# One attention unit inside a fused attention and two-layer MLP kernel: its own place table, a third softmax buffer, and products of zeros ahead of its local scores

## The chip, the cores and the metric

The program runs on one core of one Trainium2 chip. The metric is device microseconds of one execution. The kernel before was timed three times: median 927.83 us, from 927.24 to 928.4. One more execution was taken with the hardware profiler: 926.6 us, of which the span from its first to its last instruction is 924.7 us. All rows below come from that execution.

## The reference

Inputs are `q`, `k`, `v` of shape (4, 8, 576, 64) and four float32 weight matrices. The attention has a part over means of 4 positions, repeated 4 times, and a part over a band of 7 positions. Two gated MLPs follow, on 2304 tokens of 512 features with 2048 hidden features.

```python
def attn(q, k, v):                       # B=4, H=8, S=576, D=64
    q_d, k_d, v_d = (a.reshape(B, H, S // 4, 4, D).mean(axis=3) for a in (q, k, v))
    out_up = np.repeat(sm_attn(q_d, k_d, v_d), 4, axis=2)
    mask = np.abs(pos[:, None] - pos[None, :]) < 4
    scores = np.where(mask, scale * q @ k.T, -1e9)
    out_local = softmax(scores) @ v
    return out_up + out_local

x = attn(q, k, v)                        # as 2304 x 512
h = x @ w1_in;  x = (h * sigmoid(h)) @ w1_out
h = x @ w2_in;  out = (h * clip(h + 3, 0, 6) / 6) @ w2_out
```

## The kernel before, in words

The 2304 tokens are cut into eight units of 288 (half a batch element each). A matrix product in float32 is made of three products of split operands: each operand is a high part and a low part in a reduced form of float32, and high x high, low x high and high x low are added. The splitting costs ScalarE (ACT, the high part by a cast), VectorE (DVE) and GpSimd (POOL, the low part by a subtraction).

**First layer.** A row `f` (a block of 128 hidden features, 16 in all) of a unit is `gemm1` (tile `h`, 12 products of 288 columns), then `gate1` (ACT and DVE, tile `t`), then `split_g` (ACT `gh`, POOL `gl`), and two rows later `y_unit1` (tile `y`, 12 products into four accumulators). The first two units are run in an odd order: unit 0 rows 0 to 7, unit 1 rows 0 to 15, unit 0 rows 8 to 15. The four accumulators `ys` are the four buffers of the PSUM pool `ps_y`. All other products, those of attention too, go through the four buffers of `ps_w`.

**Weights.** While these first passes run, the weights of the first layer are still arriving and are converted on the chip: per tile of 128x1024 words, ACT makes `wu`, POOL or ACT makes `wt`, DVE joins them (`wt<-wu,wt`), ACT casts the high part `w` and POOL subtracts the low part (`w<-wt,w`). One conversion step is issued per place in the row loop, behind the marks of an earlier row (`gates`). The MLP products need these tiles in order.

**Attention of the next unit, listed by places.** Each row `f` has two places (`nxt[2 * i]` behind `split_g`, `nxt[2 * i + 1]` behind the `y` products). `attention(u, n, at, ...)` fills them from a table: `ATT` for units 1 and 2, `ATT_LATE` for later ones, with `at` turning a table position into a place. The pieces are: `ls` local scores (32-column products, tile `ls`), `le` and `ln` the local softmax, `lt` and `lp` its transposes into `xo`, `ds`/`dx`/`dn` scores and softmax of the mean part (tiles `ds`, `de`, `dr`), `dt` its transposes (`deT`), `dv` its values (`od`), and `lv` the local values with the final sum `x`. Unit 1's attention runs over unit 0's rows 0 to 7, that is over 16 places; before, by `ATT` with

```python
    first_att = attention(1, 2 * HF, lambda p: 1 + p * 12 // 22)
```

so that `ls` stood in places 1 and 2, `dt` in 5 to 9, `dv` in 7 and 9, `lv` in 10, 11 and 13. At row 7 `split_x` makes unit 1's operand `xhl` from `x`.

**Buffers.** Softmax results `de` and their transposes `deT` of unit 1 share the tag `de` with three buffers. The tag `stg` has two buffers; unit 0 uses them for `leT`, unit 2 for its `q` and `k` loads (`qkraw`).

**What sets the order.** The framework's scheduler orders each engine's instructions by a simulated timeline within the limits the program sets (`issue_after`, `behind`, `in_line`). An engine then runs its list strictly in order. All loads and stores are issued on SyncE's queue (SP), in order too: an issue that waits for a buffer holds back those behind it. Line 31 is the recording helper through which ACT, DVE and POOL instructions go, line 339 the one for products.

**Products of zeros.** In the prologue `keep_warm` puts products of a tile of zeros (tile `idle`) between attention pieces. The kernel before has none after the prologue.

Of the kernel before, what the change touches and what calls it, by code (L numbers as in the profile page):

```python
# [8 lines left out]
F32 = mybir.dt.float32  # L9
F32R = mybir.dt.float32r  # L10
U32 = mybir.dt.uint32
BF16 = mybir.dt.bfloat16
# [26 lines left out]
def attention_moe_moe2_kernel(  # L39
# [11 lines left out]
    nc = tc.nc  # L51
# [3 lines left out]
    P = 128  # L55
    NC = DM // P
    NF = DFF // P
    UT = S // 2
# [3 lines left out]
    SD = S // FACTOR  # L62
    UD = UT // FACTOR
# [9 lines left out]
    pool = ctx.enter_context(tc.tile_pool(name="pool", bufs=1))  # L73
# [18 lines left out]
    def parts(tag, *shapes):  # L92

        sizes = [a * b for a, b in shapes]
        t = pool.tile([P, sum(sizes)], F32, tag=tag, name=tag, bufs=1)
        at = [sum(sizes[:i]) for i in range(len(sizes))]
        return [t[:, i:i + a * b].rearrange("p (a b) -> p a b", a=a) for i, (a, b) in zip(at, shapes)]

    kT, qT, kd = parts("xe", (NC, KW), (NC, QW), (NC, SD))
# [236 lines left out]
    latest = [None]  # L336
# [4 lines left out]
    def in_line():  # L341

        return tc.issue_after(latest[0])
# [102 lines left out]
    def down_scores(u, ch):  # L446

        ss = []
        own = u == 0 and ch == 1
        for par in range(2):  # L450
            ps = (ps_y if own else ps_w).tile([P, 512], F32, tag="y" if own else "w", name="ds")
            ss.append(ps[:UD, :2 * SD].rearrange("p (c j) -> p c j", c=2))
        for c in range(2):
            for par in range(2):
                rows = slice(64 * par, 64 * par + 64)
                mm(
                    ss[par][:, c, :], qd[rows, 2 * ch + c, :], kd[rows, 2 * ch + c, :],
                    start=True, stop=True,
                )
        return ss  # L460

    def down_exp(u, i, s):
        m = pool.tile([UD, 2, 1], F32, tag="dm", name="dm", bufs=4)
        vec.tensor_reduce(out=m, in_=s, axis=AX.X, op=ALU.max)
        sc = scale / (FACTOR * FACTOR)
        vec.tensor_scalar(out=m, in0=m, scalar1=-sc, scalar2=None, op0=ALU.mult)
        if u == 0:
            e = pool.tile([UD, 2, SD], F32, tag=("gh", "gl")[i % 2], name="de", bufs=2)
        else:
            e = pool.tile([UD, 2, SD], F32, tag="de" if u < 3 else "wt", name="de", bufs=3)  # L470
        r = pool.tile([UD, 2, 1], F32, tag="dr", name="dr", bufs=4)
        for c in range(2):
            act.activation(e[:, c, :], s[:, c, :], AF.Exp, bias=m[:, c, :], scale=sc, accum_out=r[:, c, :])
        return e, r

    def down_norm(eng, e, r):
        vec.tensor_scalar(
            out=r, in0=r, scalar1=EPS, scalar2=float(FACTOR), op0=ALU.add, op1=ALU.mult
        )
        vec.reciprocal(r, r)  # L480
        eng.tensor_tensor(out=e, in0=e, in1=r.to_broadcast([UD, 2, SD]), op=ALU.mult)
# [72 lines left out]
    def local_spread(par, t, a, turning=False):  # L554

        rows = slice(32 * a, 32 * a + 32)
        copy = act.copy if a % 2 or turning else vec.tensor_copy
        copy(pT[rows, par * NC * G:(par + 1) * NC * G, QB * a:QB * (a + 1)], t[rows, :, 0:QB])
# [20 lines left out]
    def split_x0(g):  # L579
# [4 lines left out]
        act.copy(hi, s)  # L584
        vec.tensor_tensor(out=lo, in0=s, in1=hi.bitcast(F32), op=ALU.subtract)

    xs = {}
    NPOS = 2 * NF

    def attention_calls(u):  # L590

        st = {}
        local_engines = ((vec, vec), (gps, gps), (vec, vec))[min(u, 2)]
        down_engines = (gps, gps)

        def begin():
            st["od"] = pool.tile([P, NC, UD], F32, tag="od", name="od", bufs=1)
            if u == 0:
                xhl[0] = pool.tile([P, 2, NC, UT], F32R, tag="xhl", name="xhl", bufs=1)
                xs[0] = st["x"] = pool.tile([P, NC, UT], F32, tag="x32", name="x32", bufs=1)  # L600

        def ds(ch): st["ds", 2 * ch], st["ds", 2 * ch + 1] = down_scores(u, ch)
        def dx(i): st["e", i] = down_exp(u, i, st["ds", i])
        def dn(i): down_norm(down_engines[i // 2], *st["e", i])
        def dt(i): st["eT", i] = down_transpose(st["e", i][0])
        def dv(ch): down_values(u, ch, [st["eT", 2 * ch + par] for par in range(2)], st["od"])
        def ls(c): local_scores(u, st.setdefault("ls", []), c)
        def le(i): st["le", i] = local_exp(local_engines[i], u, st["ls"][i])
        def ln(i): local_norm(local_engines[i] if u else vec, st["le", i])
        def lt(i): st["leT", i] = local_transpose(u, st["le", i])  # L610
        def lp(i, a): local_spread(i, st["leT", i], a, u == 0 and i == 0)
        def lv(g):
            if u and g == 0:
                xs[u] = st["x"] = pool.tile([P, NC, UT], F32, tag="x32", name="x32", bufs=1)
            local_values(u, g, st["od"], st["x"])

        return dict(begin=begin, ds=ds, dx=dx, dn=dn, dt=dt, dv=dv, ls=ls, le=le, ln=ln, lt=lt, lp=lp, lv=lv)

    VALUES = (1, 3, 5, 7, 9, 11, 16, 18)

# [3 lines left out]
    def attention(u, n, at, ahead=None, after=17):  # L624

        names = attention_calls(u)
        places = [[] for _ in range(n)]
        first = at(0)
        for p, calls in (ATT_LATE if u > 2 else ATT).items():
            for name, *args in calls:  # L630
                places[at(p)].append((names[name], args))
        if u == 1:
            for i in range(4 * G):
                places[0].append((load_vw, (u, i // 4, i % 4)))
        if u > 1:
            prep = []
            if u % 2 == 0:
                for i in range(NC):
                    prep += [[(load_qk, (u, i)), (prep_k, (i,)), (prep_q, (i,))]]
                for h in range(H):  # L640
                    prep += [[(load_vd, (u // 2, h)), (prep_vd, (u // 2, h))]]
            else:
                prep = [[(load_qk, (u, i)), (prep_q, (i,))] for i in range(NC)]
            if u == 2:

                for p, calls in zip((10, 12), prep):
                    places[p].append((held, calls[:1]))
                for p, calls, then in zip(THIRD, prep, prep[2:] + [[], []]):
                    places[p].append((held, calls[1:] + then[:1]))
                prep = []  # L650
            start = 0
            if ahead is not None:

                for i in range(NC):
                    load, *turns = prep.pop(0)
                    ahead[after + 3 * i].append(load)
                    ahead[after + 3 + 3 * i].append((queued, turns))
                for i, (load, turn_v) in enumerate(prep):
                    if i < 2:
                        ahead[30 + i].append(load)  # L660
                    else:
                        places[VALUES[i - 2]].append(load)
                    places[VALUES[i]].append((queued, [turn_v]))
                prep = []
            for i, calls in enumerate(prep):
                places[start + i * (first - start) // len(prep)].append((held, calls))
            for i in range(4 * G):
                places[i * first // (4 * G)].append((load_vw, (u, i // 4, i % 4)))
        return places
# [11 lines left out]
    def held(*calls):  # L681
# [3 lines left out]
    ATT = {  # L685
        0: [("begin",), ("ls", 0)],
        1: [("ls", 1)],
        2: [("ls", 2)],
        3: [("ls", 3)],
        4: [("le", 0)],  # L690
        5: [("le", 1), ("ds", 0)],
        6: [("dx", 0), ("dx", 1), ("ln", 0)],
        7: [("dn", 0), ("ln", 1)],
# [11 lines left out]
        22: [("lv", 2)],  # L705
    }


    ATT_LATE = {
        0: [("begin",), ("ls", 0)],  # L710
# [223 lines left out]
    def split(i):  # L934
        split_w(0, *order[i])
        done.add((0, *order[i]))

    names = attention_calls(0)
    def keep_x():
        nc.sync.dma_start(x0d, xs[0])  # L940
# [93 lines left out]

    HF = NF // 2
    passes = [(0, range(HF)), (1, range(NF)), (0, range(HF, NF))] + [(u, range(NF)) for u in range(2, NU)]
    first_att = attention(1, 2 * HF, lambda p: 1 + p * 12 // 22)
    for c in range(2, NC):
        first_att[0].insert(0, (late_q, (c, qn1[c // 2])))
    first_att[0].sort(key=lambda call: call[0] is not late_q)  # L1040
# [13 lines left out]

    for n_pass, ((u, fs), nxt) in enumerate(zip(passes, nxts)):
        ys = [ps_y.tile([P, 512], F32, tag="y", name="y") for _ in range(NC)]
        ys = [y[:, :UT] for y in ys]
        x = xhl[u]
        end = {0: end_half1, 2: end_half2}.get(n_pass, end_unit1)
# [149 lines left out]
    for at in range(n_q):  # L1209
        u, p = divmod(at, HP)  # L1210
        n = sizes[u]
# [72 lines left out]
```

## Time and profile before

| | |
|---|---|
| median of 3 runs | 927.83 us (927.24 to 928.4) |
| profiled execution | 926.6 us, its span 924.7 us |
| PE busy | 902.3 us, 98% of the span |
| PE weight loads busy | 830.1 us, 90% |
| DVE, ACT, POOL busy | 481.9, 415.4, 351.0 us |
| share of PE on the chain that ended last | 89% |

A busy PE is not a PE at its peak: its instructions are pipelined, and its clock has two levels, 2.4 GHz (granted clock 1.00 in the rows) and 1.2 GHz (0.50). What a wait or a slow clock is worth has to be read in the stretch where it stands, since an engine that catches up later gives nothing to the end. Idle time is shown in brackets behind a row, with the engine and tile whose signal came last.

### The profile page before, as it was taken

How to read it: one execution, taken by the hardware profiler on the slowest of the kernel's cores; microseconds unless marked ns; L12 is line 12 of the kernel's file. 1: busy time of each engine (PE TensorE's matmuls, PEld its weight loads, DVE VectorE, ACT ScalarE, POOL GpSimd, SP SyncE). 2: the span in 40 equal slices, each digit the busy share in tenths (PEclk: the TensorE clock that was granted, in tenths of full speed). 3: DMA queues.
4: the chain of work that ended last, by engine and by line, in shares of the span. 5: the costliest groups of instructions: out<-in, count | busy, mean ns of one | idle time of the engine just before them, and what ended most of it. 6: DMA issues, size and time to landing. Idle time of an engine off the chain costs nothing.

```text
span 924.7 us, 20977 instructions
## 1 busy us (share of the span) xinstructions
PE 902.3 (98%) x8231; PEld 830.1 (90%) x8231; DVE 481.9 (52%) x986; ACT 415.4 (45%) x973; POOL 351.0 (38%) x457
## 2 busy tenths in 40 slices
PE   7989899999999999999999999999999999999998
PEld 4778798999999999999999998888898888888896
DVE  4874368455455364643634655555446444644422
ACT  5678635335444354443534554343325224322432
POOL 6678952225464353663346633341006003200100
PEclk9889999999999999999999999999999999999999
DMA  8979653535857758565359997667658656754580
GB/s 207 301 228 284 200 125 84 125 93 145 254 173 207 198 158 242 184 203 187 132 187 354 382 363 211 183 206 229 180 168 252 191 173 182 238 175 145 162 271 23
DMA packets 218474, 185.07 MB, mean 200 GB/s; under 512 B 90120, under 2 KB 200968, under 8 KB 218376
## 3 DMA queue, kind: packets, MB, share of 16 engines
q1 hardware_dynamic: 218376, 183.74, 65.8%
q8 instruction: 65, 1.06, 0.5%
q14 instruction: 33, 0.27, 0.1%
HBM read 154.21 MB, written 29.49 MB: 199 GB/s over the span
## 4 chain that ended last, share of the span: by engine, by line
PE 89%; DVE 4%; POOL 3%; ACT 2%; issue 1%; DMA 1%; SPq 0%; POOLq 0%; ACTq 0%; DVEq 0%
PE y L339 41%; PE h L339 20%; PE m L339 19%; PE lv L339 2%; PE ls L339 2%; PE idle L783 1%; PE dv L339 1%; PE ds L339 1%; PE dt L346 1%; PE nt L339 1%; DMA wcd<-chi 1%; POOL wt L31 1%; POOL w L31 1%; ACT t L31 0%; DVE xo L31 0%
## 5 line engine op out<-in xcount | busy, mean ns | idle before, releaser
L339 PE MATMUL h<-xhl,w 128*128 128x288 f32 x1536 | 230.9, 300 | 3.2 <-DVE t L31 1.3
L339 PE MATMUL y<-gh,w 128*128 128x288 f32 x1024 | 226.1, 298 | 1.5 <-ACT gh L31 0.5
L339 PEld LDWEIGHTS h<-xhl,w 128*128 128x128 f32 x1536 | 211.2, 190 | 8.8 <-DVE t L31 1.7
L339 PE MATMUL y<-w,g 128*128 128x512 f32 x864 | 215.7, 397 | 0.9 <-DVE g L31 0.5
L339 PEld LDWEIGHTS y<-w,g 128*128 128x128 f32 x864 | 156.3, 188 | 35.1 <-DVE g L31 2.4
L339 PEld LDWEIGHTS y<-gh,w 128*128 128x128 f32 x1024 | 171.0, 189 | 4.2 <-ACT t L31 1.2
L31 DVE SCALAR_TENSOR_TENSOR t<-t,h 128x288 f32<-128x288 f32 (+1 forms) x192 | 101.7, 532 | 128.4 <-ACT t L31 127.9
L31 POOL TENSOR_TENSOR gl<-t,gh 128x288 fp32r<-128x288 f32 x112 | 93.5, 835 | 181.6 <-ACT gh L31 167.3
L339 PE MATMUL y<-gl,w 128*128 128x288 f32 x512 | 149.6, 298 | 3.6 <-POOL qkraw L31 1.5
L339 PEld LDWEIGHTS y<-gl,w 128*128 128x128 f32 x512 | 96.3, 188 | 4.7 <-POOL qkraw L31 1.7
L31 ACT ACTIVATE t<-h 128x288 f32<-128x288 f32 x128 | 52.2, 408 | 98.7 <-PE h L339 88.4
L31 ACT CAST gh<-t 128x288 fp32r<-128x288 f32 x128 | 55.4, 433 | 85.4 <-PE y L339 62.1
L339 PEld LDWEIGHTS m<-xa,ring 128*128 128x128 f32 x720 | 90.2, 188 | 3.4
L339 PE MATMUL m<-xa,ring 128*128 128x256 f32 x720 | 91.9, 279 | 0.0
L339 PEld LDWEIGHTS m<-xb,ring 128*128 128x128 f32 x624 | 78.5, 188 | 4.1 <-DVE h L31 0.4
L31 ACT ACTIVATE t<-m,three 128x256 f32<-128x256 f32 x48 | 22.8, 474 | 129.9 <-PE m L339 126.5
L339 PE MATMUL m<-xb,ring 128*128 128x256 f32 x624 | 80.0, 280 | 0.0
L31 POOL TENSOR_TENSOR w<-wt,w 128x512 fp32r<-128x512 f32 x48 | 61.9, 1301 | 43.6 <-ACT w L31 37.0
L31 DVE SCALAR_TENSOR_TENSOR t<-t,m 128x256 f32<-128x256 f32 x48 | 20.2, 421 | 110.1 <-ACT t L31 110.1
L31 POOL TENSOR_TENSOR xa<-xsum,xa 128x512 fp32r<-128x512 f32 x9 | 12.1, 1343 | 151.9 <-ACT xa L31 151.9
L31 DVE TENSOR_TENSOR g<-t,g 128x512 fp32r<-128x512 f32 (+1 forms) x80 | 60.1, 759 | 6.2 <-ACT g L31 3.0
L31 ACT ACTIVATE t<-h,three 128x256 f32<-128x256 f32 x64 | 36.0, 610 | 41.3 <-DVE h L31 41.2
(96 smaller groups left out, 1035.3 us busy)
## 6 DMA issues: line engine op xcount, KB each, us to landing
ring<-wcd SPq DMA_DIRECT2D x120, 512.0 KB
w<-wsd SPq DMA_DIRECT2D x44, 512.0 KB
raw<-in_moe_w_out_dram SPq DMA_DIRECT2D x32, 512.0 KB
raw<-in_moe_w_in_dram SPq DMA_DIRECT2D x16, 512.0 KB
craw<-in_moe_w_in_dram SPq DMA_DIRECT2D x32, 256.0 KB
sevenths<-wcd SPq DMA_DIRECT2D x32, 256.0 KB
wcd<-chi SPq DMA_DIRECT2D x16, 448.0 KB
wcd<-comb SPq DMA_DIRECT2D x16, 448.0 KB
```

Of the source, the lines that this page charges most:

```text
L31: r = getattr(self.engine, name)(*args, **kwargs)
L339: latest[0] = nc.tensor.matmul(*args, **kwargs).ins
L346: latest[0] = nc.tensor.transpose(*args).ins
L783: nc.tensor.matmul(ps[:, :n_cols], z[:, :P], z[:, :n_cols], start=True, stop=True)
```

## The change

Unit 1 gets a table of its own, `ATT_FIRST`, whose positions are places as they are (`lambda p: p`). `ls`, `le`, `ds 0`, `dx 0`, `dx 1`, `ln` keep the places they had. `dx 2` moves from 5 to 6, `dx 3` from 7 to 6, `dt` from 5, 6, 8, 9 to 6, 7, 9, 10, `dv` from 7, 9 to 9, 11, `lv` from 10, 11, 13 to 12, 13, 13. Unit 1's softmax results 2 and 3 go into the two buffers of `stg`. Ahead of the first `ls`, seven products of 224 columns are issued on a zero column of `kT`, which is read as bf16 and broadcast; they write columns 288 to 511 of the first accumulator's PSUM buffer, which nothing else uses.

```diff
         if u == 0:
             e = pool.tile([UD, 2, SD], F32, tag=("gh", "gl")[i % 2], name="de", bufs=2)
+        elif u == 1 and i > 1:
+            e = pool.tile([UD, 2, SD], F32, tag="stg", name="de", bufs=2)
         else:
...
+        def fill(n):
+            z = kT[:, 0, 0:1].bitcast(BF16)[:, 0:1]
+            with in_line():
+                for _ in range(n):
+                    latest[0] = nc.tensor.matmul(
+                        spare[0], z.to_broadcast([P, P]), z.to_broadcast([P, 512 - UT]), start=True, stop=True
+                    ).ins
...
-        for p, calls in (ATT_LATE if u > 2 else ATT).items():
+        for p, calls in (ATT_LATE if u > 2 else ATT_FIRST if u == 1 else ATT).items():
...
+    ATT_FIRST = {
+        1: [("begin",), ("fill", 7), ("ls", 0), ("ls", 1)],
...
+        6: [("dx", 2), ("dx", 3), ("dt", 0), ("lp", 0, 2), ("lp", 0, 3)],
...
-    first_att = attention(1, 2 * HF, lambda p: 1 + p * 12 // 22)
+    first_att = attention(1, 2 * HF, lambda p: p)
...
         ys = [ps_y.tile([P, 512], F32, tag="y", name="y") for _ in range(NC)]
+        spare[:] = [ys[0][:, UT:]]
         ys = [y[:, :UT] for y in ys]
```

On PE, at the start of unit 0's row loop (`nt` are transposes of unit 1's `q`, the first `h` is row 0, the next row 1), before:

```order
L339 MATMUL h<-xhl,w 128x288 x4
L339 MATMUL nt<-ident,nat 64x72 x6
L339 MATMUL ls<-xe 32x32 x48
L339 MATMUL y<-gh,w 128x288 x4
L339 MATMUL ls<-xe 32x32 x26
L339 MATMUL h<-xhl,w 128x288 x12
L339 MATMUL ls<-xe 32x32 x22
```

and now, where of the seven pairs of rows on line 621 the first and the last stand:

```order
L339 MATMUL h<-xhl,w 128x288 x4
L339 MATMUL nt<-ident,nat 64x72 x6
L621 LDWEIGHTS xe
L621 MATMUL y<-xe 128x224
...
L339 MATMUL ls<-xe 32x32 x48
L339 MATMUL y<-gh,w 128x288 x4
L339 MATMUL ls<-xe 32x32 x13
L339 MATMUL h<-xhl,w 128x288 x12
L339 MATMUL ls<-xe 32x32 x35
```

The zero products stand between the transposes and the first 48 local scores; of the other 48, 13 stay ahead of row 1's `h` where 26 did.

On DVE, around the gate of row 2 (`t<-t,h`) and the first softmax of the mean part (`dm` its maxima, `dr` its sums):

```order
 L31 TENSOR_SCALAR dm<-dm 72x2 x2
-L31 SCALAR_TENSOR_TENSOR t<-t,h 128x288
...
+L31 TENSOR_SCALAR dr<-dr 72x2
+L31 RECIPROCAL dr<-dr 72x2
+L31 TENSOR_SCALAR dr<-dr 72x2
+L31 TENSOR_REDUCE dm<-ds 72x2
+L31 RECIPROCAL dr<-dr 72x2
 L31 TENSOR_REDUCE lr<-le 128x12
+L31 TENSOR_REDUCE dm<-ds 72x2
+L31 TENSOR_SCALAR dm<-dm 72x2
+L31 SCALAR_TENSOR_TENSOR t<-t,h 128x288
```

The gate stood in front of the sums and now stands behind them and behind the maxima of the second pair of softmaxes. On PE the `h` of row 3 moves the other way: it stood behind the 12 `y` products and a `dt` of row 2, and now stands ahead of them, right behind the second `ds`.

On PE, around the transposes and the values of the mean part (the second `h` of the rows before is row 4's), before:

```order
L339 MATMUL h<-xhl,w 128x288 x12
L346 MATMUL dt<-ident,de 72x72 x4
L339 MATMUL dv<-deT,vd 64x72 x8
L339 MATMUL h<-xhl,w 128x288 x12
L339 MATMUL y<-gh,w 128x288 x4
L339 MATMUL y<-gl,w 128x288 x4
L346 MATMUL dt<-ident,de 72x72 x4
L339 MATMUL y<-gh,w 128x288 x4
```

and now:

```order
L346 MATMUL dt<-ident,de 72x72 x4
L339 MATMUL h<-xhl,w 128x288 x12
L339 MATMUL dv<-deT,vd 64x72 x8
L346 MATMUL dt<-ident,de 72x72 x4
L339 MATMUL y<-gh,w 128x288 x4
L339 MATMUL y<-gl,w 128x288 x4
L339 MATMUL h<-xhl,w 128x288 x12
L346 MATMUL dt<-ident,de 72x72 x4
```

Between the second transposes and the values that read their copy stands now a whole `h`, where nothing stood. On SP the first four `q` loads of unit 2 move from ahead of unit 1's `v` loads to behind the next weight loads, one of them ahead of three such loads and three behind these, since their buffer is now held by a softmax result.

## Rows read from the trace of the kernel before

**Rows 1.** The page: PE's granted clock, in tenths, in 40 slices of the span.

```profile
PEclk9889999999999999999999999999999999999999
```

**Rows 2.** Busy time by stretch: PE, PEld, DVE, ACT, POOL; clock; DMA share; GB/s.

```profile
39.60:43.00 3.40, 2.17 (x97) 1.81 (x99) 3.06 (x7) 2.33 (x6) 2.55 (x3) 1.00 1.04 374
43.00:49.80 6.80, 6.80 (x153) 6.05 (x139) 3.02 (x6) 3.84 (x8) 5.38 (x6) 0.51 1.07 344
49.80:63.40 13.60, 10.90 (x83) 8.96 (x82) 11.92 (x31) 10.37 (x30) 11.29 (x16) 1.00 0.76 211
63.40:66.80 3.40, 3.40 (x24) 3.26 (x25) 1.69 (x5) 2.45 (x6) 1.00 (x5) 0.52 0.55 213
...
83.40:112.50 29.10, 24.01 (x171) 22.58 (x170) 10.66 (x21) 20.40 (x44) 27.46 (x33) 1.00 0.66 209
112.50:154.00 41.50, 41.50 (x483) 39.14 (x481) 30.95 (x73) 19.95 (x54) 20.19 (x26) 1.00 0.48 111
```

**Rows 3.** Timeline of PE: start, us, line, operation, count, idle before it.

```profile
27.35 1.51 PE L783 MATMUL idle<-zeros 128*128 128x224 bf16 x14
...
42.72 0.73 PE L339 MATMUL ls<-xe 64*32 64x32 f32 x48 [1.00 <-DVE t L31]
43.38 1.33 PE L339 MATMUL y<-gh,w 128*128 128x288 f32 x4
...
45.35 3.25 PE L339 MATMUL h<-xhl,w 128*128 128x288 f32 x12
...
51.42 1.85 PE L339 MATMUL h<-xhl,w 128*128 128x288 f32 x12
53.11 0.69 PE L339 MATMUL y<-gh,w 128*128 128x288 f32 x4
...
59.05 1.85 PE L339 MATMUL h<-xhl,w 128*128 128x288 f32 x12
...
63.37 1.09 PE L339 MATMUL dv<-deT,vd 72*64 72x72 f32 x14 [0.86 <-ACT deT L31]
64.40 3.00 PE L339 MATMUL h<-xhl,w 128*128 128x288 f32 x12
...
111.67 0.40 PE L339 MATMUL y<-gl,w 128*128 128x288 f32 x1 [1.50 <-POOL qkraw L31]
```

**Rows 4.** Timeline of POOL, the same columns.

```profile
50.08 0.80 POOL L31 TENSOR_TENSOR gl<-t,gh 128x288 fp32r<-128x288 f32 x1 [1.36 <-DMA qkraw<-in_q_dram]
...
54.55 1.29 POOL L31 TENSOR_TENSOR w<-wt,w 128x512 fp32r<-128x512 f32 x1
...
65.71 0.81 POOL L31 TENSOR_TENSOR gl<-t,gh 128x288 fp32r<-128x288 f32 x1 [2.52 <-ACT gh L31]
...
83.39 1.31 POOL L31 TENSOR_TENSOR w<-wt,w 128x512 fp32r<-128x512 f32 x1 [1.44 <-ACT w L31]
...
90.46 0.64 POOL L31 TENSOR_SCALAR wt<-raw 128x512 uint32<-128x512 uint8 x1
```

**Rows 5.** Timeline of DVE, the same columns.

```profile
47.37 0.69 DVE L31 SCALAR_TENSOR_TENSOR wt<-wu,wt 128x512 uint32<-128x512 uint32 x1 [1.55 <-POOL wt L31]
49.08 0.45 DVE L31 SCALAR_TENSOR_TENSOR t<-t,h 128x288 f32<-128x288 f32 x1 [1.01 <-ACT t L31]
...
54.99 0.88 DVE L31 TENSOR_SCALAR dr<-dr 72x2 f32<-72x2 f32 x1 [0.78 <-ACT de L31]
```

**Rows 6.** DVE from 49 to 65 us by instruction: busy us, mean ns; idle.

```profile
L31 DVE TENSOR_SCALAR dr<-dr 72x2 f32<-72x2 f32 x3 | 3.0, 986 | 0.8 <-ACT de L31 0.8
...
L31 DVE TENSOR_REDUCE dm<-ds 72x2 f32<-72x288 f32 x4 | 1.7, 443 | 0.1
...
L31 DVE TENSOR_REDUCE lr<-le 128x12 f32<-128x384 f32 x2 | 1.0, 516 | 0.0
```

**Rows 7.** Timeline of SP's queue.

```profile
43.00 3.64 SPq L352 DMA_DIRECT2D qkraw<-in_q_dram  x4
...
66.58 0.33 SPq L157 DMA_DIRECT2D raw<-in_moe_w_out_dram  x1
```

More of the change, by code (lines that the diff above doesn't have):

```diff
@@ L585, in split_x0 @@
         vec.tensor_tensor(out=lo, in0=s, in1=hi.bitcast(F32), op=ALU.subtract)
+    spare = []
     xs = {}
@@ L615, in lv @@
             local_values(u, g, st["od"], st["x"])
-        return dict(begin=begin, ds=ds, dx=dx, dn=dn, dt=dt, dv=dv, ls=ls, le=le, ln=ln, lt=lt, lp=lp, lv=lv)
+        return dict(begin=begin, ds=ds, dx=dx, dn=dn, dt=dt, dv=dv, ls=ls, le=le, ln=ln, lt=lt, lp=lp, lv=lv, fill=fill)
     VALUES = (1, 3, 5, 7, 9, 11, 16, 18)
@@ L705, in attention_moe_moe2_kernel @@
         22: [("lv", 2)],
+    }
+    ATT_FIRST = {
[13 rows of a table added]
     }
```

11 rows, old and new, of the table ATT_FIRST are left out of this document.

## The prediction, made before the changed kernel was run

> **What bounds the kernel now.** I read the slices of the clock first, then the busy times by stretch, then the timelines of PE, POOL and DVE around the places that the change touches.
>
> In the slices [rows 1] the reader is to see that PE's clock is at its upper level everywhere but in the first slices, each 23.1 us long. So whatever the change can win or lose lies in the first tenth of the span. The busy times by stretch [rows 2] show why it matters in two ways. From 112.5 to 154 us PE is busy for all of 41.50 us at full clock: work that reaches PE earlier there ends earlier, and the end follows. From 83.4 to 112.5 PE is busy for 24.01 of 29.10 us, so it stands still for 5.09 us, while POOL is busy for 27.46 of 29.10. There POOL sets the pace, with its subtractions for weights and for `gl`; the last of these waits, 1.50 us at 111.67 [rows 3], hands the pace back to PE. A microsecond won on PE before 83 us is therefore worth something only as far as POOL's closed run starts earlier. That is how I size every term: by the gaps of POOL and of the engines that feed it, not by PE's own time.
>
> Before that run lie two stretches at 1.2 GHz: 43.0 to 49.8 (granted clock 0.51) and 63.4 to 66.8 (0.52) [rows 2]. Ahead of the first fall PE ran transposes and 32-column products and stood still for 1.00 us; ahead of the second it stood still several times, last for 0.86 us before the `dv` products [rows 3].
>
> **The change part by part.**
>
> *Seven products of zeros.* The prologue runs 14 of the same size in 1.51 us at full clock [rows 3], 0.108 each, so seven take 0.76 us. They stand between the transposes and the first local scores, and behind those PE now waits 1.00 us for the gate of row 0 (`t`), which is on DVE and does not depend on them. So 0.76 goes into that wait: cost 0. Were the wait gone, it would cost 0.76, at half clock twice that.
>
> *The first slow stretch.* What it costs PE: four `y` products took 1.33 us against 0.69 at full clock, and the 12 of `h` 3.25 against 1.85 [rows 3], together 2.04. I take it that the zero products hold the clock here. What reaches POOL is less. The row 1 `gl` at 50.08 came 1.36 us after POOL ran out of work [rows 4], and the gate in front of it on DVE stood behind an idle 1.01 us, while the instruction before that gate on DVE itself waited 1.55 us for POOL's `wt` [rows 5]. So the gate can come at most 1.01 earlier. Bounds 0 and 1.36; I take 1.0, the DVE row being the nearest link.
>
> *The second slow stretch.* The `h` at 64.40 took 3.00 us against 1.85, so 1.15 is lost to the clock, and POOL's `gl` at 65.71 stands behind an idle 2.52 us [rows 3, 4]. The new order puts a whole `h` between the second transposes and the values that read their copy, which is the cover for the 0.86 us wait at 63.37; with it the reason for the fall lessens. From 49.8 to 63.4 DVE was busy for 11.92 of 13.60 us [rows 2], so most of that POOL gap is DVE's queue and stays. Bounds 0 and 2.52; I take 1.2, about the part that the clock took.
>
> *Waits of `dt` and `dv` themselves.* They go, but they are PE's, and PE has 5.09 us to spare later. Counted 0; as much as 0.9 if it were PE that set the pace.
>
> *The third and fourth softmax.* They no longer wait for one of the three `de` buffers, so `dx 3` comes earlier and `dn` with it. POOL does the same products in another order: 0. Where it adds something is DVE's order: two scalings of sums `dr`, two maxima and one sum `lr` now stand ahead of the gate of row 2, 2 x 0.986 + 2 x 0.443 + 0.516 = 3.37 us [rows 6], and row 3's `h`, now right behind the second `ds`, waits for that gate. Hidden behind it is the `y` work that stood ahead of that `h`: in before 53.27 to 59.05 passed between the end of row 2's `h` and the start of row 3's [rows 3], in which 12 `y` products and a `dt` of row 2 ran that now come after. Wait and moved work are of like size, so 0; bounds -1.0 and +2.5.
>
> *The `lv` products two places later.* `x` has to be there for `split_x` at row 7, whose place and last `lv` are as before. The casts of `xhl` also wait for row 7's own `h`, so one more DVE addition stands beside that: 0, at most 0.5.
>
> *The `q` loads of unit 2.* 3.64 us of SP's queue at 43.0 move behind later weight loads [rows 7], and one of them now waits until a softmax buffer has been read, with the loads issued at 66.58 behind it. Those are the weights of steps 19 to 21, and POOL converts step 19 at 90.46 [rows 4], 24 us later. A wait of a few us is hidden: 0.
>
> The sum: 1.0 + 1.2 = 2.2 us off. The profiled execution took 926.6 us, so 924.4; the median of the runs shown, 927.83, lies 1.23 above it, and the forecast for the median is 927.8 - 2.2 = 925.6.
>
> A rule that speaks against the new order: two of the instructions moved ahead of the gate are scalings of a 72x2 tile, which took 0.986 us on average though they touch two columns. The one at 54.99 ended at 55.87, and POOL's `w` of 54.55 ended at 55.84 [rows 4, 5]. The Trainium skill, "SBUF — State Buffer", section "Who interferes with whom", says that VectorE and GpSimd share a port pair as an exclusive lock and that the one that comes second "fully blocks" for the whole instruction. The trace agrees. By that rule the two scalings could each wait out a whole POOL subtraction of 1.29 us, and the sum would be 2 x (1.29 - 0.99) = 0.6 us worse, 926.2.
>
> **The rivals.**
>
> *POOL swallows it.* POOL's closed run starts at 83.39 behind 1.44 us of idle, for a cast on ACT [rows 4]. If ACT, which also has the softmax exponentials and copies, gets to that cast no earlier, the run starts when it did, and PE waits longer in front of it. For: ACT was busy 10.37 of 13.60 us and POOL 27.46 of 29.10 [rows 2]. Against: the two gaps of 1.36 and 2.52 are really PE's doing. Time: about 0.5 us off, 927.3.
>
> *The zeros don't hold the clock.* They run, and the clock falls all the same, here or a few us on. For: they are 0.76 us beside 32-column products that stay. Against: in the prologue such products stand between pieces of attention, at full clock [rows 3]. What remains is the second term, 1.2, or less: 926.8.
>
> *More than that.* The gaps of POOL at 50.08, 65.71 and 83.39 add up to 5.3 us [rows 4]; if engines that get their input earlier close nearly all of them, about 5 us go: 922.8. Against: DVE and ACT are full for most of that time.
>
> *Slower: the gate of row 2 comes last.* Row 3's `h` waits on PE for a gate behind 3.37 us of DVE work, some of it locked against POOL. PE then stands still long enough for the clock to fall right there, and `h` and the `y` products behind it run at half clock: 1.40 and 0.64 by the rows of the first slow stretch, about 2.0 us, on top of a wait that exceeds the moved work by up to 2.5. This decides if the gate comes more than about 2 us after the second `ds`. With 2.2 us won elsewhere it is 2.0 + 2.5 - 2.2 = 2.3 us slower: 930.1.
>
> **How the numbers follow.** The forecast 0.43, of which 0.37 is faster; the larger gain 0.15; swallowed 0.19, the clock not held 0.08, both within the bound for most; slower 0.15. About 0.2% of the time, 1.86 us, is what a measurement of this kernel can tell from no change. So faster 0.37 + 0.15 = 0.52; same 0.06 + 0.19 + 0.08 - 0.02 = 0.31; slower 0.15 + 0.02 = 0.17. The range has to reach the larger gain and most of the slower case: 922.4 to 929.2. The forecast's own range is 924.4 to 926.6.
>
> **What would show it.** Right: the clock at 1.00 from 41 to 52 us, row 1's `h` near 1.85 instead of 3.25, and the zero products inside the wait that ended at 42.72; POOL's gap before row 1's `gl` well under 1.36; no slow stretch around 64 us; POOL's closed run beginning some 2 us earlier, and from there to the end the same kernel shifted. Wrong: a slow stretch that begins between 50 and 60 us with PE waiting for DVE's gate in front of row 3's `h`; or a closed run that begins where it did, with PE's idle time in it grown by what was won before; or waits for SP's weight loads, which I put at nothing.

## The result, and the profile after

The forecast was 925.6 us. The changed kernel took 935.29 us (median of 5 runs, 931.28 to 937.4) against 927.83 before (5 runs, 927.04 to 928.4): ratio 1.0070, 95% interval 1.0046 to 1.0093. A second set of 6 runs gave 932.28 (931.05 to 933.9) against 926.9 (17 runs), ratio 1.0052, 1.0034 to 1.0070. So it is 5 to 7.5 us slower, beyond the range of the prediction. The profiled execution took 936.61 us, its span 934.5.

Which part of the span that is. The prologue's code is the same, but the first product `h` started at 39.02 us against 37.01 before; over all profiles of this study it lay between 36.5 and 41.1 us, in another profile of the same changed kernel at 37.83. These 2 us lie within that spread and are taken as chance. From the last four products of row 0's `h` to the `y` that waits for POOL's `gl` near 100 us, 58.48 us passed before (39.83 to 98.31) and 64.30 after (41.83 to 106.13). This stretch is called D below. In these two profiles it holds 5.8 of the 9.8 us between the spans. Its two ends, before and after:

```profile
39.83 0.80 PE L339 MATMUL h<-xhl,w 128*128 128x288 f32 x4 [0.72 <-DVE xhl L31]
98.31 0.40 PE L339 MATMUL y<-gl,w 128*128 128x288 f32 x1 [1.26 <-POOL gl L31]
```

```profile
41.83 0.80 PE L339 MATMUL h<-xhl,w 128*128 128x288 f32 x4 [0.72 <-DVE xhl L31]
106.13 0.40 PE L339 MATMUL y<-gl,w 128*128 128x288 f32 x1 [1.30 <-POOL gl L31]
```

PE's timeline after, with the rows that answer to [rows 3] (start, us, line, operation, count, idle before it):

```profile
43.09 0.86 PE L621 MATMUL y<-xe 128*128 128x224 bf16 x7
44.72 0.67 PE L339 MATMUL ls<-xe 64*32 64x32 f32 x54 [0.27 <-DVE t L31]
45.34 0.80 PE L339 MATMUL y<-gh,w 128*128 128x288 f32 x4
46.94 1.85 PE L339 MATMUL h<-xhl,w 128*128 128x288 f32 x12 [0.15 <-DVE xo L31]
48.72 0.77 PE L339 MATMUL ls<-xe 64*32 64x32 f32 x67
51.88 0.32 PE L339 MATMUL ls<-xe 64*32 64x32 f32 x3 [2.39 <-issue]
...
56.65 2.50 PE L339 MATMUL h<-xhl,w 128*128 128x288 f32 x12
62.70 1.85 PE L339 MATMUL h<-xhl,w 128*128 128x288 f32 x12 [1.85 <-DVE t L31]
66.50 1.83 PE L339 MATMUL h<-xhl,w 128*128 128x288 f32 x12
70.17 0.72 PE L339 MATMUL dv<-deT,vd 72*64 72x72 f32 x16 [1.83 <-DVE t L31]
73.94 3.25 PE L339 MATMUL h<-xhl,w 128*128 128x288 f32 x12 [1.33 <-ACT deT L31]
...
118.86 0.40 PE L339 MATMUL y<-gl,w 128*128 128x288 f32 x1 [1.84 <-POOL qkraw L31]
```

The first five rows are the forecast: the zeros fill the wait (0.27 left of 1.00), the four `y` take 0.80 instead of 1.33, row 1's `h` 1.85 instead of 3.25. Then comes what was not forecast: 2.39 us of "issue", that is, of waiting for nothing that the profile shows, three records before the end of the local scores; a wait for row 2's gate `t` (1.85), one for row 3's gate in front of `dv` (1.83), and a row 5 `h` at half clock.

The stretches of [rows 2], after (busy time of PE, PEld, DVE, ACT, POOL; clock; DMA share; GB/s):

```profile
43.00:49.80 6.80, 5.77 (x218) 4.72 (x214) 3.70 (x8) 5.13 (x11) 6.32 (x7) 1.00 1.11 343
49.80:63.40 13.60, 9.67 (x56) 8.53 (x56) 7.51 (x24) 6.88 (x22) 7.83 (x9) 0.75 0.32 87
63.40:66.80 3.40, 3.40 (x31) 3.36 (x30) 3.38 (x8) 3.08 (x10) 3.19 (x8) 1.00 0.27 57
66.80:83.40 16.60, 13.44 (x113) 11.99 (x112) 8.92 (x16) 11.83 (x27) 12.02 (x22) 0.79 0.96 324
83.40:112.50 29.10, 25.42 (x205) 24.10 (x202) 13.92 (x24) 20.56 (x46) 24.17 (x30) 1.00 0.85 249
112.50:154.00 41.50, 39.66 (x452) 37.47 (x451) 25.70 (x56) 18.86 (x43) 24.25 (x31) 0.96 0.44 102
```

The row of 66.8 to 83.4 us before, which [rows 2] leave out:

```profile
66.80:83.40 16.60, 16.25 (x157) 14.67 (x157) 9.80 (x20) 14.12 (x34) 13.60 (x24) 1.00 0.95 301
```

The clock is up where it was down (43 to 49.8 us) and down where it was up (0.75 and 0.79 in the second and fourth row). POOL, busy for 11.29 us of the second stretch before [rows 2], is busy for 7.83 (7.93 if the stretch is moved by the 2 us of the late start), and for 12.02 instead of 13.60 in the fourth.

Some of the loss lies behind D. The wait for POOL's `qkraw`, 1.50 us before [rows 3], is 1.84 at 118.86, and the clock falls behind it: from 112.5 to 154 us its mean is 0.96, where it was 1.00. If only the two levels occur, that is 0.04 x 41.5 = 1.7 us of PE's time, an estimate. The second profile of the changed kernel (e15, below) has the same fall and spends 60.9 us in D: there D holds 2.4 of the 5.5 us between the spans (930.2 and 924.7). The fall is also in e4, which loses nothing that can be told from chance, so it is not shown how much it counts.

DVE after, around the gate of row 3, the last row; and POOL around the same time:

```profile
65.41 2.62 DVE L31 TENSOR_SCALAR dr<-dr 72x2 f32<-72x2 f32 x1
67.94 0.57 DVE L31 STREAM_TRANSPOSE leT<-le 128x384 f32<-128x384 f32 x1
...
68.54 0.99 DVE L31 COPY xo<-leT 32x288 f32<-32x288 f32 x2
69.56 0.46 DVE L31 SCALAR_TENSOR_TENSOR t<-t,h 128x288 f32<-128x288 f32 x1
```

```profile
50.97 0.80 POOL L31 TENSOR_TENSOR gl<-t,gh 128x288 fp32r<-128x288 f32 x1 [0.27 <-ACT gh L31]
57.77 1.29 POOL L31 TENSOR_TENSOR w<-wt,w 128x512 fp32r<-128x512 f32 x1 [2.32 <-ACT w L31]
...
64.36 0.17 POOL L31 MEMSET raw<- 128x1 uint32 x3
...
65.27 0.67 POOL L31 TENSOR_TENSOR de<-de,dr 72x288 f32<-72x288 f32 x1
65.90 0.84 POOL L31 TENSOR_TENSOR le<-le,lr 128x384 f32<-128x384 f32 x1
66.69 1.32 POOL L31 TENSOR_TENSOR w<-wt,w 128x512 fp32r<-128x512 f32 x1
```

Row 3's `h` ended at 64.55 us (62.70 + 1.85); its gate began at 69.56. What stood ahead of it on DVE was a transpose, two copies, and before these a scaling of two columns, which took 2.62 us: it ended at 68.03 with POOL's `w` (66.69 + 1.32 = 68.01), at the end of three POOL products that followed each other without a gap. Before row 1's `gl`, POOL's gap is 0.27 instead of the 1.36 of [rows 4].

### The profile page after: what moved, and what is told of

Same layout as the page of the kernel before. It is cut to its first block, busy times and chain, and to the rows that moved or that the text cites. A ratio compares the mean times of both kernels' runs of the same rounds, so it can differ in the third digit from the quotient of the medians.

```text
span 934.5 us, 20992 instructions
## 1 busy us (share of the span) xinstructions
PE 907.8 (97%) x8238; PEld 835.2 (89%) x8238; DVE 483.6 (52%) x986; ACT 415.3 (44%) x973; POOL 350.6 (38%) x457
## 3 DMA queue, kind: packets, MB, share of 16 engines
q8 instruction: 65, 1.06, 0.5%
## 4 chain that ended last, share of the span: by engine, by line
PE 86%; DVE 5%; POOL 3%; issue 2%; ACT 2%; DMA 1%; SPq 0%; POOLq 0%; DVEq 0%; ACTq 0%
PE y L339 40%; PE m L339 19%; PE h L339 19%; PE lv L339 2%; PE ls L339 2%; PE idle L813 2%; PE dv L339 1%; PE ds L339 1%; POOL w L31 1%; PE dt L346 1%; PE nt L339 1%; POOL wt L31 1%; DMA wcd<-chi 1%; DVE t L31 1%; DVE xhl L31 1%
## 5 line engine op out<-in xcount | busy, mean ns | idle before, releaser
L31 ACT CAST gh<-t 128x288 fp32r<-128x288 f32 x128 | 55.4, 432 | 86.7 <-PE y L339 60.9
```

Source lines behind the costliest of these rows:

```text
L31: r = getattr(self.engine, name)(*args, **kwargs)
```

## The experiments

All 16 kernels (e15 is the changed one again), with D as above, the start of row 3's gate counted from the same product of row 0, and how far that gate starts behind the end of row 3's `h` (all three from one profile each):

| kernel | median us (runs) | ratio to before, 95% | D | gate 3 | behind `h` |
|---|---|---|---|---|---|
| before | 926.9 to 927.8 | 1 | 58.5 | 24.4 | 3.3 |
| changed | 935.29 (5) | 1.0070 (1.0046, 1.0093) | 64.3 | 27.7 | 5.0 |
| e15 changed again | 932.28 (6) | 1.0052 (1.0034, 1.0070) | 60.9 | 24.5 | 5.0 |
| e1 no zeros | 927.17 (12) | 1.0002 (0.9986, 1.0019) | 57.1 | 19.9 | 3.2 |
| e2 zeros alone | 929.01 (12) | 1.0020 (1.0003, 1.0036) | 58.4 | 24.4 | 2.7 |
| e3 own buffers | 931.87 (8) | 1.0049 (1.0030, 1.0068) | 59.0 | 20.7 | 1.1 |
| e4 stg alone | 928.36 (12) | 1.0010 (0.9993, 1.0027) | 57.2 | 24.7 | 3.1 |
| e5 five zeros | 931.23 (9) | 1.0039 (1.0023, 1.0054) | 59.3 | 22.7 | 3.7 |
| e6 gate 2 behind | 927.17 (12) | 0.9994 (0.9980, 1.0008) | 57.6 | 21.3 | 0.9 |
| e7 late v | 932.34 (8) | 1.0049 (1.0032, 1.0066) | 60.2 | 24.2 | 4.7 |
| e8 table alone | 933.56 (6) | 1.0066 (1.0047, 1.0085) | 63.1 | 20.6 | 2.9 |
| e9 quiet transfers | 926.04 (12) | 0.9981 (0.9969, 0.9994) | 55.1 | 19.0 | 1.0 |
| e10 no zeros, late v | 926.74 (12) | 0.9991 (0.9976, 1.0007) | 57.7 | 21.4 | 3.7 |
| e11 zeros behind | 933.53 (7) | 1.0054 (1.0030, 1.0078) | 61.2 | 24.7 | 5.0 |
| e12 gate 3 first | 928.66 (12) | 1.0013 (0.9999, 1.0028) | 59.0 | 22.6 | 1.0 |
| e13 quiet, no zeros | 927.60 (12) | 0.9995 (0.9981, 1.0008) | 56.0 | 19.7 | 3.2 |
| e14 late gate 3 | 931.30 (12) | 1.0037 (1.0021, 1.0054) | 61.5 | 24.6 | 7.0 |

The kernel before itself lies anywhere from 924.1 to 931.3 us in 117 runs of these sessions, so a difference under 1.5 us is read only where the interval of its ratio leaves out 1.

Where row 3's gate came 4.7 us or more behind its `h`, the kernel lost, every time (the changed one in both sets, e7, e11, e14). Three kernels lost with that gate at 3.7 us or less (e3, e5, e8), so it isn't the only way to lose.

**The parts of the change (e1 to e4, e8).** In the expectations, theories 1 and B are the same: the stop in the local scores and the clock are the loss. Theories 2 and A put it on row 2's gate, theory 3 on the late start, and theory C, from e12 on, on row 3's gate.

```diff
# e1: the changed kernel without zeros (e8: also without stg)
-        1: [("begin",), ("fill", 7), ("ls", 0), ("ls", 1)],
+        1: [("begin",), ("ls", 0), ("ls", 1)],
# e2: before, its table with fill 7 ahead of ls 0.   e4: before, with the stg lines
# e3: the changed kernel without the stg lines
```

> The changed kernel without its seven products of zeros: table and buffers stay. Theory 1 (the zeros are the loss: with the clock held up PE runs through the local scores so fast that it stands 2.39 us at 49.5 us with no wait that the profile names, and its clock falls behind that, 2.4 + about 2.9 us): the first slow stretch is back at 43 to 50 us, no stop of over 1 us in the local scores, and the time is 926 to 930 us. Theory 2 (the table is the loss: row 3's product waits for row 2's gate behind the softmax's DVE work, raw's buffers come free 7 us later): 932 to 937 us, the waits of 1.8 us at row 3's h and at dv stay. Theory 3 (the prologue, whose code is the same, happened to run 2 us later in the profiled execution, and that is chance): about 2 us of the 7.5 are no property of the kernel, and this run's spread shows it.

> The kernel before with the seven products of zeros ahead of its first local scores, and nothing else of the change. Theory 1: PE stands over 1 us without a named wait in the local scores behind the zeros, the clock falls after it, and the time is 931 to 936 us. Theory 2: the zeros win what the prediction gave them or nothing, 926 to 928 us.

> The changed kernel, but unit 1's softmax results 2 and 3 stay in the three buffers of de: zeros and table alone. Both theories: the softmax results wait for buffers again, within 2 us of the changed kernel, 933 to 938 us. If the loss sits in SP's queue, since unit 2's loads of q now wait for a softmax result: 926 to 930 us, and the load of raw issued at 64.5 us is at 58 us again.

> The kernel before with unit 1's softmax results 2 and 3 in the two buffers of stg, and nothing else of the change: the loads of q of unit 2 wait for them. If the loss sits in SP's queue: 931 to 935 us. Theories 1 and 2: 927 to 929 us, since the data of these loads is not needed for another 20 us.

> The table alone: no zeros, and the softmax results stay in de's three buffers. Both theories: no loss, 926 to 929 us; if the third buffer is what lets the table gain, 928 to 930 us, otherwise as the table with the buffers, about 927 us.

Table and buffers without zeros cost nothing that can be told from chance (e1), nor do the buffers alone (e4); the zeros alone cost 0.2% (e2). Together they cost 0.5 to 0.7%. So the loss is no sum of the parts. Zeros and table without the `stg` lines (e3) were expected at 933 to 938 us, or at 926 to 930 if SP's queue were the loss, and took 931.87: the `stg` buffers are not what the changed kernel loses by. What e3 loses by is open; D holds only 0.5 us of it, and its row 3's gate is early. The table alone without the two `stg` buffers (e8) was expected between 926 and 930 and lost as much as the whole change: the table needs the buffers. Its profile shows PE in front of `dt`, for a `wt` that stood on DVE behind copies `xo` of 2.65 and 2.06 us, and then at half clock up to 78 us:

```profile
69.66 0.69 PE L346 MATMUL dt<-ident,de 72*72 72x72 f32 x4 [3.43 <-DVE wt L31]
```

What ties the zeros to the rest is the scheduler. With seven zeros it writes another order for all engines. In e1, as before, DVE has row 2's gate ahead of the first scalings `dr`; with seven zeros it stands behind them. Row 3's gate stands in e1 ahead of the first two copies `xo` and of the second transpose; with seven zeros it stands behind the copies, and in the kernel before it stood behind both. DVE in e1, then before:

```profile
60.49 0.42 DVE L31 SCALAR_TENSOR_TENSOR t<-t,h 128x288 f32<-128x288 f32 x1
60.84 3.55 DVE L31 COPY xo<-leT 32x288 f32<-32x288 f32 x2
```

```profile
62.04 1.63 DVE L31 COPY xo<-leT 32x288 f32<-32x288 f32 x2
...
64.20 0.41 DVE L31 SCALAR_TENSOR_TENSOR t<-t,h 128x288 f32<-128x288 f32 x1
```

So row 3's gate had copies ahead of it before too; new is the scaling of 2.62 us in front of these. The orders shown ahead of the prediction have the move of row 2's gate, but there it had been put down to the table.

**Row 2's gate or the clock? (e5, e6, e7).**

```diff
# e5
-        1: [("begin",), ("fill", 7), ...
+        1: [("begin",), ("fill", 5), ...
# e6: no zeros; dx 0, dx 1, dn 0, dn 1 at place 3, and in gate1
+        with tc.issue_after(sums_now[0]) if sums_now[0] is not None else ExitStack():
             vec.scalar_tensor_tensor(out=t, ...)
# e7: v's loads wait for a memset on POOL behind row 1's gl
-                places[0].append((load_vw, (u, i // 4, i % 4)))
+            places[3].append((held, [(gps.memset, (vw[:, :, 0, 0:1], 0.0))]))
+                places[3].append((held, [(load_vw, (u, i // 4, i % 4))]))
```

> The changed kernel with five zero products instead of seven. With five the scheduler leaves the gate of row 2 on DVE ahead of the first softmax's scalings, as it does without zeros; with seven it stands behind them. Theory A (the zeros cost through the order: the gate of row 2 comes last): row 3's h waits well under 1.8 us and the time is 926 to 929 us, though PE may stand in the local scores. Theory B (the zeros cost through the clock: PE at full clock runs out of the local scores' stream, stands 2.4 us, and the clock falls): the stop and the fall are there as with seven, 932 to 936 us.

> The changed kernel without zeros, but with the gate of row 2 held behind the first two scalings on DVE by an order that the program sets: the first softmax of the mean part is listed one place earlier and the gate is issued after its scalings. Theory A: row 3's h waits 1.5 to 2 us for the gate, and the time is 930 to 934 us. Theory B: no stop in the local scores and the time is that without zeros, 926 to 929 us.

> The changed kernel, seven zeros, with the order of PE, DVE and ACT as it was, but unit 1's twelve loads of v are held by a memset on POOL behind row 1's subtraction, so that SP's transfers end before PE comes to the last local scores. Theory B with its cause in the transfers (PE's instructions arrive late while the DMA engines are full): the stop of 2.4 us in the local scores goes, the clock stays up to row 2, and the time falls by 2 to 5 us, to 930 to 933 us. Theory A: the gate of row 2 is as late behind its softmax, row 3's h still waits about 1.8 us, and the time stays at 934 to 937 us.

e6 settles row 2's gate: behind its scalings, with the expected wait and the clock down in row 3's `h`, and no loss (927.17).

```profile
56.77 2.87 PE L340 MATMUL h<-xhl,w 128*128 128x288 f32 x12 [1.85 <-DVE t L31]
```

Theory A as it was put then fell with this run. e5 lost 0.4% with row 2's gate in front, which spoke for theory B, but its profile also has PE wait 2.04 us in front of `dt`, for a `wt` on DVE behind copies that took 3.34 us, as e8's does. e7, with the stop at 1.67 us and not gone, ended where the second set of the changed kernel did (932.3), which spoke for neither.

**Order alone, and one gate alone (e11, e12, e14).** e11 has the changed kernel's order on every engine; only the zeros stand 48 scores later, where they cover no wait.

```diff
# e11
-        1: [("begin",), ("fill", 7), ("ls", 0), ("ls", 1)],
+        1: [("begin",), ("ls", 0), ("ls", 1), ("fill", 7)],
# e12: the changed kernel; lt 0, lp 0 and dn 3 listed with row 3; lt 0 is held the same way
+            with tc.issue_after(gated_now[0]) if u == 1 and i > 1 else ExitStack():
                 down_norm(down_engines[i // 2], *st["e", i])
# e14: e1, with row 3's gate behind the two copies that followed it
+        with tc.issue_after(copied[0]) if copied[0] is not None else ExitStack():
             vec.scalar_tensor_tensor(out=t, ...)
```

> The changed kernel, with the same order on every engine, but the seven zeros stand behind the first 48 local scores instead of ahead of them. They no longer cover the wait for the gate of row 0, so PE stands 1.0 us there as before and the clock falls as before; the zeros themselves then cost PE 0.8 to 1.5 us. Theory B: at half clock there is no stop over 1 us in the local scores, and the time is 927 to 931 us. Theory A (it is the order that the zeros bring about): the gate of row 2 stands behind its softmax as in the changed kernel, and the time stays at 934 to 937 us.

> The changed kernel with seven zeros ahead of the local scores and the same order up to DVE's second join in that stretch, but from there the gate of row 3 is held ahead of the second softmax's scalings and of the first local transpose. In the changed kernel that gate came at 69.56 us, 5 us behind row 3's h, since a scaling that took 2.62 us, a transpose and two copies stood ahead of it on DVE. Theory C (this gate is the larger loss): the wait of 1.83 us in front of dv goes, POOL's weights come earlier, and the time falls to 928 to 931 us although the stop of about 2 us in the local scores stays. Theory B (the stop and the fall of the clock behind it are the whole loss): 933 to 936 us.

> The table and buffers without zeros, which took 927.2 us, with one swap on DVE: the gate of row 3 is held behind the two copies of the first local transpose into xo that followed it (3.55 us together there, locked against POOL). PE's and POOL's order stays as it was to the last instruction. Theory C (the late gate of row 3 is the larger loss by itself): PE waits 3 to 5 us more in front of what follows, the clock falls there, and the time is 930 to 933 us. If the gate only costs together with the other things that the zeros bring (the stop, the fall of the clock): 927 to 929 us.

In e11 PE stood 1.01 us at row 0's gate, the clock fell behind that wait as before (0.67 from 44 to 46 us, 0.50 from 46 to 48), the stop was 0.86 us, and from 50 to 68 us the clock was up. It lost all the same. Its PE and DVE (in two fences) have the changed kernel's rows again:

```profile
51.62 0.25 PE L339 MATMUL ls<-xe 64*32 64x32 f32 x3 [0.86 <-issue]
59.63 1.85 PE L339 MATMUL h<-xhl,w 128*128 128x288 f32 x12 [1.85 <-DVE t L31]
67.08 0.72 PE L339 MATMUL dv<-deT,vd 72*64 72x72 f32 x16 [1.83 <-DVE t L31]
70.86 3.25 PE L339 MATMUL h<-xhl,w 128*128 128x288 f32 x12 [1.05 <-ACT deT L31]
```

```profile
62.33 2.62 DVE L31 TENSOR_SCALAR dr<-dr 72x2 f32<-72x2 f32 x1
...
66.48 0.45 DVE L31 SCALAR_TENSOR_TENSOR t<-t,h 128x288 f32<-128x288 f32 x1
```

So the clock and the stop are not the larger loss. e12 leaves zeros, stop and row 2's gate as they are and takes row 3's gate out from behind the scaling of 2.62 us (PE, then DVE):

```profile
50.58 0.25 PE L340 MATMUL ls<-xe 64*32 64x32 f32 x3 [1.92 <-issue]
60.08 2.51 PE L340 MATMUL h<-xhl,w 128*128 128x288 f32 x12 [1.85 <-DVE t L31]
```

```profile
63.61 0.45 DVE L31 SCALAR_TENSOR_TENSOR t<-t,h 128x288 f32<-128x288 f32 x1 [0.80 <-ACT t L31]
...
64.48 0.35 DVE L31 TENSOR_SCALAR dr<-dr 72x2 f32<-72x2 f32 x2
```

Two scalings now take 0.35 us together, the wait of 1.83 in front of `dv` is gone, and the kernel takes 928.66: of the loss of 5 to 7.5 us some 1 us is left. (The edit moves the second softmax's scalings and the first transpose along with the gate, so it is not the gate alone.) e14 goes the other way, from the version that loses nothing, with PE's and POOL's order unchanged:

```profile
63.96 3.18 DVE L31 COPY xo<-leT 32x288 f32<-32x288 f32 x2
67.17 0.45 DVE L31 SCALAR_TENSOR_TENSOR t<-t,h 128x288 f32<-128x288 f32 x1
```

```profile
67.68 3.25 PE L340 MATMUL h<-xhl,w 128*128 128x288 f32 x12 [4.63 <-DVE t L31]
```

It takes 931.30 where e1 took 927.17: ratio 1.0037 against 1.0002. Row 3's gate, put behind DVE work that is held up beside POOL, is enough for most of the loss, and taking it out from there takes most of it away. In both pairs (e1 and e14, e12 and e11 or e15) the intervals of the two ratios don't overlap. The column of gate 3 by itself isn't a rule: before, the gate came as late (24.4) as in e11, e14 and e15, but row 3's `h` ended later there too (21.1 against 19.7, 17.7 and 19.5), and in e5 and e8 another wait came last.

**The transfers, and what zeros are worth (e9, e10, e13).** In e9 `v`, the last two weight loads of the prologue and the store of `x0` all wait behind row 1's `gl`; e13 is e9 without zeros, e10 is e1 with e7's edit.

```diff
# e9: e7's edit, and behind it (the loads leave their old places):
+        for o in order[14:16]:
+            load_w(0, *o, hold=True)
+        with tc.issue_after(v_last[0]):
+            nc.sync.dma_start(x0d, xs[0])
```

> The changed kernel with seven zeros; the loads of v, the last two weight loads of the prologue and the store of x0 are all held behind row 1's subtraction on POOL, so that the DMA engines have nothing to move when PE comes to the last local scores. PE's order is as in the changed kernel up to row 3; the gate of row 2 stands behind the first scalings. Theory B with its cause in the transfers: the stop in the local scores shrinks below 0.8 us (2.39 with full DMA engines, 1.67 with v held alone), the clock stays at 1.00 from 41 to 58 us, and the time is 927 to 931 us. If the stop does not come from the transfers it stays near 1.7 us, and the time near 932 us.

> The table and the buffers without zeros, and unit 1's loads of v held behind row 1's subtraction on POOL. If holding v helps only by way of the stop that zeros bring about: no gain over the table without zeros, 926.5 to 928.5 us. If holding v helps by itself (it frees the DMA engines for the weights): 923 to 926 us, faster than both.

> The version with the quiet transfers (v, two weight loads and x0's store behind row 1's subtraction) without its seven zeros. If the zeros pay once PE's instructions arrive in time and the gates stay early, it is slower than with them, by the 1.0 us that the prediction gave them or more: 927 to 928 us against 926.0. If the quiet transfers alone made that version fast: 925 to 926 us, and zeros are worth nothing.

e9 beats both kernels: 926.04 us, 0.19% under before (0.06 to 0.31%). Its order has row 3's gate early (58.87 us, 1.0 us behind its `h` and ahead of the transpose at 59.48). PE's clock, and its stop:

```profile
PEclk9999999999999999999999999999999999999999
```

```profile
48.65 0.25 PE L339 MATMUL ls<-xe 64*32 64x32 f32 x3 [1.14 <-issue]
```

The stop was expected under 0.8 us and is 1.14. Without its zeros the same kernel takes 927.60 (e13), so the zeros bring 1.6 us there (1.3 by the ratios); the two ratios, 0.9981 and 0.9995, have intervals that overlap, so this is near the size forecast (1.0) but not shown. Holding `v` back without zeros (e10) brings nothing that can be told from chance.

**The changed kernel again (e15).**

> The changed kernel once more, beside the runs of the kernel before on the same chip. All theories: 933 to 937 us; the stop in the local scores is there again with 1.9 to 2.5 us, and so is the scaling of 2.6 us ahead of the gate of row 3. If the first row's start at 39.0 us (37.0 before, with the same code up to there) was chance, it lies anywhere between 36.4 and 41 us in this profile.

The time, 932.28 us, is just under the range that was expected, and the stop, which came again, is shorter (1.63 us). The 2.62 us scaling ahead of row 3's gate is there as well, and so is the 1.83 us wait in front of `dv`. The late prologue is not, nor is the half clock from 52 to 58 us behind the stop. That is the difference between the two sets as far as one profile each can tell.

## Why the prediction was wrong, step by step

*The zeros (0.76 us inside a wait: cost 0).* On PE this was right: they took 0.86 us, and the wait behind them shrank from 1.00 to 0.27. What failed is the assumption under it, that zeros act on PE alone. The scheduler counts them too, and orders every engine behind them anew.

*The step that failed: the third and fourth softmax and DVE's order, "so 0; bounds -1.0 and +2.5".* It ascribed DVE's order to the table, named row 2's gate as the one to watch, and summed the instructions ahead of it, 3.37 us, at their durations before [rows 6]. Those instructions took 2.19 us, less than was counted, and row 2's gate costs nothing (e6). The one that costs is row 3's, of which the sum has nothing. It stands behind a transpose, two copies and a scaling that took 2.62 us, where its like was counted at 0.986, and it came 5.0 us after the end of its `h`, where it was 3.3 before. By the ratios the late gate is worth 3.2 us alone (e1 to e14, 0.35%) and 3.6 or 3.8 in the changed kernel (e15 or e11 to e12, 0.39 or 0.41%), more than the bound of 2.5. How it gets on: `dv` waits for the gate's `t` (1.83), row 5's `h` behind it for a copy on ACT (1.33), the clock falls in that `h` (3.25 instead of 1.85), and POOL, which was already behind, does 12.02 instead of 13.60 us of work from 66.8 to 83.4. That `dv` needs the buffer of `ps_w` which row 3's `h` holds until its gate has read it, follows from the code; the trace names only `t`.

The rule cited there, the Trainium skill's "SBUF — State Buffer", section "Who interferes with whom", was weighed at 0.6 us: one whole POOL subtraction per scaling. The trace agrees that DVE is held up beside POOL, but not for one instruction: here for 2.62 us, to the end of a run of POOL products without a gap, and in e14 for 3.18 us in two copies. The Trainium skill's "SBUF — State Buffer", section "Who interferes with whom", ties the lock to certain kinds of VectorE instructions; no row here names the kind. Before the change one scaling at 56.34 us already took 1.41, more than one subtraction, which the mean of 0.986 hid.

*First slow stretch (1.0).* Gone, as forecast: clock 1.00, POOL's gap 0.27. But a new one, from 52 to 58 us, came behind the stop. The gain shows only where row 3's gate is early (e13 to e9, 1.6 us, not shown).

*Second slow stretch (1.2).* Not gone but moved, to 72 to 78 us, behind the wait for row 3's gate. In e9, with that gate early, it is gone.

*Waits of dt and dv.* `dv`'s 0.86 us became 1.83, on another releaser. *lv later, q loads (0).* Right: e1 and e4 have them and cost nothing. But the weight loads that now stand ahead of them on SP came at 64.49 instead of 57.8 us, since POOL reached their memset late (64.36); SP's row:

```profile
64.49 0.39 SPq L152 DMA_DIRECT2D raw<-in_moe_w_in_dram  x1
```

*The rivals.* The slower one, 930.1 at 0.15, had the kind of mechanism right (a gate behind locked softmax work, the clock falling behind the wait) and the place wrong; its threshold, row 2's gate 2 us after the second `ds`, was nearly met in e6 without loss (56.29, 1.4 us behind the end of the second `ds`, as in the changed kernel). The first sign of being wrong came in both its halves, by luck: the slow stretch began at 52 us behind the stop, and PE's wait for row 2's gate (1.85) came behind that stretch, at full clock. And the loss is not all in the first tenth of the span, where the prediction looked: the fall of the clock behind 118.86 lies outside. A rival that the change's parts act on each other through the scheduler was missing.

## What to carry to other kernels

When a scheduler orders the program, an inserted instruction is an edit to every engine: compare the orders of the kernel with and without each part, not only of before and after, and ascribe each move to its part. Follow every gate of the pipeline through the moved region, not just the first one, and price DVE work beside POOL by the length of POOL's run without a gap rather than by its mean. Then pin the one instruction that must not fall back; that was worth 3 to 4 us here.

## What the runs showed that was not expected

PE's stop sits at a fixed count of instructions. With seven zeros it came three records before the end of the local scores in all eight profiles (changed twice, e2, e3, e7, e9, e11, e12: 0.37 to 2.39 us); with five zeros one record before the end (e5, 1.97 us), two later; without zeros in e6, 0.60 us long, in front of the fifth `y` behind them, four records past the end, seven later. Each zero fewer moves it by one product. In all ten profiles exactly 855 products are recorded ahead of it. The other kernels without zeros show no such stop.

```profile
52.89 0.19 PE L339 MATMUL ls<-xe 64*32 64x32 f32 x1 [1.97 <-issue]
```

```profile
49.37 0.29 PE L340 MATMUL y<-gl,w 128*128 128x288 f32 x1 [0.60 <-issue]
```

The DMA view of the changed kernel from 48.5 to 52 us has one packet of kind instruction beside data that fill the DMA engines:

```profile
q1 hardware_dynamic: 1436, 0.96, 108.1%
q8 instruction: 1, 0.02, 2.7%
```

The whole run has 65 such packets of together 1.06 MB, 16 KB each, and PE ran 8238 products and as many weight loads, about 253 records to a packet. The kernel before has one such packet from 48.5 to 52 us as well, beside less data (84.9%), and no stop. That PE's instructions arrive in pieces, and late where short products use them up fast and the DMA engines are full, fits the fixed count, but is not shown. The Trainium skill's "Runtime: NRT & Kernel Launch", section "Instruction fetch mechanics", describes such fetching in 16 KiB blocks of 256 instructions and calls its cost mostly hidden. The packets here agree in size; the stop of up to 2.39 us in these profiles is not hidden, if it is this fetch, which no run here proves. That fewer transfers shorten it is not shown either (1.14 us in e9 against 1.63 and 2.39 in two profiles of one kernel).
